# A pooled-attention kernel on one core: which half of k and q comes over which DMA queue in batch 0

## The chip, the core and the metric

The kernel runs on one core of a Trainium2 chip. The core has TensorE (PE in the profile; its weight loads are listed as PEld), VectorE (DVE), ScalarE (ACT), GpSimd (POOL) and SyncE (SP). PE multiplies matrices and writes to PSUM, DVE and ACT copy, cast and compute elementwise, POOL computes and issues DMAs, SP here only issues DMAs. The metric is the time of one execution on the device in microseconds; a lower time is better. The number given for a kernel is the median over its runs.

## What is computed

The inputs are q, k and v of 8 batches, 8 heads, 576 tokens and 64 values per head, all fp32, and two weights. First comes an attention in which k and v are averaged over groups of 8 tokens, so each head has 72 keys; then a feed-forward layer whose activation is h times cos(h). Cut to what matters:

```python
k_p = k.reshape(B, H, Sp, pool, D).mean(axis=3)          # 576 tokens -> 72
v_p = v.reshape(B, H, Sp, pool, D).mean(axis=3)
scores = scale * np.matmul(q, k_p.transpose(0, 1, 3, 2))
attn = np.exp(scores - np.max(scores, axis=-1, keepdims=True))
attn = attn / (np.sum(attn, axis=-1, keepdims=True) + 1e-09)
x = np.matmul(attn, v_p)                                 # -> (4608 tokens, 512)
h = x @ w_in                                             # 512 -> 2048
out = (h * np.cos(h)) @ w_out                            # 2048 -> 512
```

## The kernel before

The feed-forward layer is worked off in nine chunks of 512 tokens. Eight of them are the first 512 tokens (in an order of their own) of the eight batches, the ninth collects the 64 tokens left over from each batch. For each chunk PE computes h in PSUM (`up_mm`, line 348), ACT takes the cosine (line 355), DVE multiplies (line 358), and PE multiplies with w_out (line 361). The attention of the next batch is worked in between these products, and the loads, the pooling and the transposes of later batches run on POOL and SP meanwhile. Batch 0 has nothing to hide behind: its attention is the beginning of the kernel, and the first `up_mm` waits for it.

The instructions stand on each engine in the order in which the program text names them. No planner moves them; semaphores are set where one engine uses what another wrote. So a waiting instruction holds up everything that the text puts behind it on that engine.

What happens at the beginning, engine by engine, with lines of the profile:

- q, k and v of batch 0 are read so that a partition holds nine consecutive tokens of one head (`even_view`, line 85). 128 partitions hold two heads, and the four pairs of heads are the index j. "First half" means j = 0 and 1, "second half" j = 2 and 3. `load_even` (line 88) loads over POOL's queue and casts from fp32 to bf16 in the DMA. What comes over SP's queue is kept in fp32 and lands in a part of `g_sb`, the buffer of the activations, that nothing else uses yet.
- SP issues k's first half and k's second half (line 405), both fp32. ACT casts pair 0, DVE pairs 1, 2 and 3 (line 407) into the tile `kv_st`.
- POOL makes two small index tables (lines 413 and 416), then issues q's first half, q's second half, v's first half and v's second half (lines 418 to 421), then makes the identity matrix, then goes on with the eight loads of w_in (line 130) and with batch 1. From the ninth of its transfers on, each issue waits until the eighth before it has landed.
- DVE fills the tile of ones for the warm-up products (line 397), builds `groups`, a matrix of zeros and ones that says which token belongs to which group of eight (lines 427 to 431), and clears some tiles (lines 434 to 441).
- PE runs ten warm-up products of 512 columns whose result nobody uses (`warm_up`, line 472). Then `pool_k_mm` pools k's first half by multiplying with `groups` (line 180, 36 products), and DVE and ACT copy the result to `kk` (line 186). After three more warm-ups `q_transpose_mm` (line 231) transposes nine blocks of 128 columns of q's first half. The copies of these to `qT` go to ACT for four blocks and to DVE for five (line 232). After two more warm-ups come the scores of units 0 and 1 (`scores`, line 251): heads 0 to 3, tokens 0 to 255 and 256 to 511. ACT takes their exponentials (line 261).
- Then the same for the second halves: `pool_k_mm` of pairs 2 and 3, the transposes of blocks 9 to 17, the sums of the exponentials (line 280), the pooling of v (`pool_v_mm`, line 195, copied to `vz` in line 197), the scores of units 2 and 3, the products with v (line 289), the normalisation (lines 295, 296 and 303), and the first `up_mm`.

PSUM is used as three pairs of banks, `banks[0]` to `banks[2]`, and two single ones, `obanks[0]` and `obanks[1]`. Before, the pooled k of the first half lies in the two single ones, and the transposes of blocks 5 to 8 go to `obanks[0]` as well, those of 0 to 4 to a half of `banks[2]`.

Of the kernel before, what the change touches and what calls it, by code (L numbers as in the profile page):

```python
# [9 lines left out]
FP32 = mybir.dt.float32  # L10
# [9 lines left out]
def kernel(  # L20
# [9 lines left out]
    nc = tc.nc  # L30
    B, H, S, D = q.shape
# [5 lines left out]
    KCH = d_model // 128  # L37
    FFCH = d_ff // 128
    NT = n_tokens // TILE
    ROW = S // 64  # L40
# [24 lines left out]
    g_sb = wpool.tile([128, FFCH, TILE], BF16, name="g_sb")  # L65
# [11 lines left out]
    banks = [psum.tile([128, 2, 512], FP32, name=f"bank{i}") for i in range(3)]  # L77
    obanks = [psum.tile([128, 512], FP32, name=f"obank{i}") for i in range(2)]
# [4 lines left out]
    staged = {}  # L83

    def even_view(src, b, j0=0, j1=KCH):
        return src[b, 2 * j0:2 * j1].rearrange("(j a) (p t) d -> (a p) j (t d)", a=2, t=ROW)

    def load_even(dst, b, src, j0=0, j1=KCH):
        nc.gpsimd.dma_start(out=dst[:, j0:j1].rearrange("p j t d -> p j (t d)"), in_=even_view(src, b, j0, j1))
# [12 lines left out]
    def q_tile(b):  # L102
        staged["q", b] = qst.tile([128, KCH, ROW, D], BF16, name="q_b", tag="q_b")
# [69 lines left out]
    def pool_k_mm(b, pair, pj0, pj1):  # L173

        kb = staged["k", b]
        ps = [bank[:, 0:(pj1 - pj0) * Sp].rearrange("p (j n) -> p j n", n=Sp) for bank in pair]
        for pj in range(pj0, pj1):
            for t in range(ROW):
                for a, rows in enumerate(half):
                    nc.tensor.matmul(ps[a][rows, pj - pj0, :], lhsT=kb[rows, pj, t, :], rhs=groups[rows, t, :],  # L180
                                     start=(t == 0), stop=(t == ROW - 1))
        dst = kk[b % 2].rearrange("p (j a) n -> p j a n", a=2)

        def put(copy, a):
            for rows in half:
                copy(out=dst[rows, pj0:pj1, a, 0:Sp], in_=ps[a][half[a]])

        return [lambda copy, a=a: put(copy, a) for a in range(2)]
# [26 lines left out]
    def qT_tile(b):  # L215
        att["qT", b] = asb.tile([128, QB, 128], BF16, name="qT", tag="qT")

    def q_flat(b):
        return staged["q", b].rearrange("p j t d -> p (j t d)")
# [5 lines left out]
    def q_transpose_mm(b, bank, g0, g1):  # L225

        if ("qT", b) not in att:
            qT_tile(b)
        ps = bank.bitcast(BF16)[:, 0:(g1 - g0) * 128].rearrange("p (g n) -> p g n", n=128)
        for g in range(g0, g1):  # L230
            nc.tensor.matmul(ps[:, g - g0, :], q_flat(b)[:, g * 128:(g + 1) * 128], identity, is_transpose=True)  # L231
        return lambda copy: copy(out=att["qT", b][:, g0:g1, :], in_=ps)  # L232
# [166 lines left out]

    kv_even_tiles(0)  # L400
    q_tile(0)
    first_k = []
    k_first = g_sb.rearrange("p f n -> p (f n)").bitcast(FP32)[:, 0:KCH * ROW * D]
    for j in (0, 2):
        nc.sync.dma_start(out=k_first.rearrange("p (j n) -> p j n", j=KCH)[:, j:j + 2], in_=even_view(k, 0, j, j + 2))
    for j, copy in enumerate((nc.scalar.copy,) + (nc.vector.tensor_copy,) * 3):
        first_k.append(lambda j=j, copy=copy: copy(out=staged["k", 0][:, j].rearrange("p t d -> p (t d)"),  # L407
                                                   in_=k_first[:, j * ROW * D:(j + 1) * ROW * D]))
    first_k[0]()

    row_of = consts.tile([128, ROW], FP32, name="row_of")
    for rows in half:
# [2 lines left out]
    first_of = consts.tile([128, Sp], FP32, name="first_of")  # L415
    nc.gpsimd.iota(first_of, pattern=[[POOL, Sp]], base=0, channel_multiplier=0,
                   allow_small_or_imprecise_dtypes=True)
    load_even(staged["q", 0], 0, q, 0, 2)
    load_even(staged["q", 0], 0, q, 2, 4)
    load_even(staged["v", 0], 0, v, 0, 2)  # L420
    load_even(staged["v", 0], 0, v, 2, 4)
# [7 lines left out]
    nc.vector.scalar_tensor_tensor(out=sign, in0=dist, scalar=1.0 - POOL, in1=dist, op0=ADD,  # L429
                                   op1=mybir.AluOpType.mult)  # L430
    nc.vector.tensor_scalar(out=groups, in0=sign, scalar1=0.0, scalar2=None, op0=mybir.AluOpType.is_le)
    first_k[1]()
    ones = consts.tile([128, 32], BF16, name="ones")
    nc.vector.memset(ones, float(POOL))
    gate = consts.tile([1, 1], BF16, name="gate")
# [33 lines left out]
    def warm_up(n, bank):  # L469

        for i in range(n):
            nc.tensor.matmul(bank, lhsT=warm[:, 0:128], rhs=warm)  # L472

    vec, act = nc.vector.tensor_copy, nc.scalar.copy
    us = BY_HEADS

    def unit(bank):
        return bank.rearrange("p (q e n) -> p q e n", q=1, e=2)

    warm_up(10, banks[1][:, 0, :])  # L480
    puts = pool_k_mm(0, obanks, 0, 2)
    puts[0](vec)
    puts[1](act)
    first_k[2]()
    first_k[3]()
    warm_up(3, banks[1][:, 0, :])
    q_transpose_mm(0, obanks[0], 5, 9)(act)
    q_transpose_mm(0, banks[2][:, 0, :], 0, 5)(vec)
    warm_up(2, banks[1][:, 0, :])
    scores(0, us[0], banks[0])  # L490
    scores(0, us[1], banks[1])
# [41 lines left out]
    for t in range(NT):  # L533
# [76 lines left out]
        elif b < B:  # L610
# [5 lines left out]
            d = 2 if t == 1 else 0  # L616
# [84 lines left out]
```

## Time and profile before

The three runs took 292.49, 292.79 and 292.93 us, median 292.79. One execution was taken with the profiler; what follows is from it.

| | |
|---|---|
| the profiled execution's own time | 292.54 us |
| its span (first to last instruction) | 290.5 us |
| PE busy | 282.9 us, 97% of the span |
| DVE busy | 170.6 us, 59% |
| POOL busy | 145.5 us, 50% |
| ACT busy | 142.0 us, 49% |
| mean DMA rate | 127 GB/s |
| the first `up_mm` (line 348) starts at | 16.90 us |

Times inside the profile are counted from the start of the span. In the timeline a line has the start, the busy time, the engine, the source line, the operation, the tile written and the tiles read, the count, and in brackets the idle time of the engine before and what ended it. Landings of DMAs are listed separately, as the time from issue to landing. The busy time of pipelined products overlaps: 56 products of line 348 take 12.31 us together, though one lasts 0.379.

### The profile page before, as it was taken

Reading aid. Unit: us, or ns where it says so; the run is one execution under the profiler, and the core shown is the slowest. Engines: PE = TensorE matmul, PEld = TensorE weight load, DVE = VectorE, ACT = ScalarE, POOL = GpSimd, SP = SyncE. Lnnn points to the kernel's source line nnn. Section 1 sums busy time; section 2 is a strip of 40 time slices with the busy share of each in tenths; the row PEclk is TensorE's granted clock in tenths of the full one; section 3 lists DMA queues with packets and bytes.
Section 4 is the critical chain, followed back from the end, with each engine's and each line's share of the span. In section 5 each row is a group of like instructions: output and inputs, shape, how many; then the busy total and the mean of one; then the engine's idle time right before and its main releaser. Section 6 shows DMA issues by size and latency. Waiting matters only on the chain.

```text
span 290.5 us, 4941 instructions
## 1 busy us (share of the span) xinstructions
PE 282.9 (97%) x1991; PEld 147.1 (51%) x1991; DVE 170.6 (59%) x231; ACT 142.0 (49%) x142; POOL 145.5 (50%) x121
## 2 busy tenths in 40 slices
PE   7799999999999999999999999999999999999994
PEld 3555544555555555555555545554555455445443
DVE  5557885774747574658275737573666557217621
ACT  3686644679046903692368316850676066016400
POOL 8546928989964696479535982599000000000000
PEclk9999999999999999999999999999999999999999
DMA  7999999989677978695769866965703510230033
GB/s 203 197 202 210 206 203 193 166 148 212 120 147 106 190 111 174 101 176 109 158 78 198 126 138 118 185 128 105 144 1 73 119 38 0 53 82 11 0 72 73
DMA packets 57158, 36.89 MB, mean 127 GB/s; under 512 B 36400, under 2 KB 50928, under 8 KB 57136
## 3 DMA queue, kind: packets, MB, share of 16 engines
q0 software_dynamic: 17104, 17.77, 37.8%
q1 hardware_dynamic: 39792, 18.69, 33.2%
q8 instruction: 15, 0.25, 0.3%
q10 hardware_dynamic: 240, 0.13, 0.2%
q14 instruction: 7, 0.06, 0.1%
HBM read 36.70 MB, written 9.44 MB: 159 GB/s over the span
## 4 chain that ended last, share of the span: by engine, by line
PE 95%; DVE 2%; ACT 1%; issue 0%; DVEq 0%
PE bank L348 43%; PE obank L361 27%; PE bank L361 8%; PE obank L367 5%; PE bank L251 3%; PE bank L320 3%; PE bank L367 2%; PE bank L472 2%; PE bank L389 1%; PE bank L289 1%; ACT ex L261 1%; DVE qT L232 0%; DVE xT L303 0%; PE obank L180 0%; DVE kv_st L407 0%; PE obank L231 0%
## 5 line engine op out<-in xcount | busy, mean ns | idle before, releaser
L355 ACT ACTIVATE cos<-bank,half_pi 128x1024 f32<-128x1024 f32 x72 | 80.3, 1117 | 116.2 <-PE bank L348 116.2
L348 PE MATMUL bank<-xT,w_in_sb 128*128 128x512 bf16 x576 | 126.0, 379 | 0.0
L358 DVE TENSOR_TENSOR g_sb<-bank,cos 128x1024 bf16<-128x1024 f32 x72 | 88.1, 1224 | 49.1 <-ACT cos L355 49.0
L348 PEld LDWEIGHTS <-w_in_sb 128*128 128x128 bf16 x576 | 65.1, 113 | 59.1 <-issue 0.2
L361 PE MATMUL obank<-w_out_sb,g_sb 128*128 128x512 bf16 x360 | 83.9, 379 | 0.0
L361 PEld LDWEIGHTS <-g_sb 128*128 128x128 bf16 x462 | 41.9, 97 | 45.9 <-issue 2.0
L161 POOL TENSOR_TENSOR kv_st<-kv_st 72x2048 f32<-72x2048 bf16 (+1 forms) x13 | 50.4, 3877 | 14.0 <-DMA kv_st<-in_k_dram 13.9
L374 DVE COPY o_sb<-obank 128x512 f32<-128x512 f32 x21 | 14.4, 690 | 31.5 <-PE obank L361 25.9
L261 ACT ACTIVATE ex<-bank 72x1024 bf16<-72x1024 f32 x32 | 30.3, 1018 | 4.9 <-PE bank L251 4.9
L164 POOL TENSOR_TENSOR kv_st<-kv_st 72x1024 f32<-72x1024 f32 (+1 forms) x13 | 29.2, 2249 | 0.9
L361 PE MATMUL bank<-w_out_sb,g_sb 128*128 128x512 bf16 x102 | 27.6, 380 | 0.0
L324 DVE TENSOR_TENSOR x_r<-bank,inv_r 128x512 bf16<-128x512 f32 (+1 forms) x32 | 22.1, 689 | 1.3 <-DVE inv_r L321 0.3
L367 PE MATMUL obank<-w_out_sb,g_sb 64*128 64x512 bf16 x144 | 18.3, 376 | 0.0
L168 POOL TENSOR_TENSOR kp<-kv_st 72x512 bf16<-72x512 f32 (+1 forms) x14 | 16.1, 1169 | 0.5
L367 PEld LDWEIGHTS <-g_sb 64*128 64x128 bf16 x196 | 9.8, 94 | 7.3
L251 PE MATMUL bank<-qT,kk 64*72 64x256 bf16 (+1 forms) x184 | 13.0, 250 | 0.6 <-DVE qT L232 0.3
L251 PEld LDWEIGHTS <-kk 64*72 64x72 bf16 x192 | 8.4, 111 | 8.5 <-issue 3.8
L529 POOL COPY gate<-kk 1x1 bf16<-1x1 bf16 x5 | 0.9, 177 | 23.0 <-DMA kk<-kp 23.0
L119 POOL DMA_DIRECT2D kv_st<-in_v_dram x15 | 9.7, 661 | 4.8 <-DVE vz L171 4.5
L320 PEld LDWEIGHTS <-ex 72*128 72x128 bf16 x192 | 8.7, 97 | 6.2 <-ACT ex L261 1.7
L321 DVE RECIPROCAL inv_r<-bank 128x8 f32<-128x8 f32 (+1 forms) x32 | 6.5, 203 | 8.0 <-PE bank L320 7.5
L376 DVE COPY o_sb<-obank 128x512 f32<-128x512 f32 x6 | 4.1, 691 | 11.9 <-PE obank L367 11.9
(79 smaller groups left out, 167.0 us busy)
## 6 DMA issues: line engine op xcount, KB each, us to landing
out_dram<-o_sb SPq DMA_DIRECT2D x70, 128.0 KB, 2.4
q_b<-in_q_dram POOLq DMA_DIRECT2D x6, 576.0 KB, 8.2
kv_st<-in_k_dram POOLq DMA_DIRECT2D x6, 512.0 KB, 5.9
kv_st<-in_v_dram POOLq DMA_DIRECT2D x6, 512.0 KB, 10.0
w_in_sb<-in_moe_w_in_dram POOLq DMA_DIRECT2D x8, 256.0 KB, 10.7
w_out_sb<-in_moe_w_out_dram POOLq DMA_DIRECT2D x8, 256.0 KB, 10.1
g_sb<-in_k_dram SPq DMA_DIRECT2D x2, 576.0 KB, 4.0
q_b<-in_q_dram POOLq DMA_DIRECT2D x4, 288.0 KB, 8.8
```

What stands on the lines that cost most here:

```text
L161: add(out=s, in0=x[:, :, 0:4, :], in1=x[:, :, 4:8, :], op=ADD)
L164: add(out=s[:, :, 0:2, :], in0=s[:, :, 0:2, :], in1=s[:, :, 2:4, :], op=ADD)
L168: add(out=kp[:, h0:h1, slot, :], in0=s[:, :, 0, :], in1=s[:, :, 1, :], op=ADD)
L251: nc.tensor.matmul(ps.rearrange("p (g n) -> p g n", n=64), lhsT=kk[b % 2][half[r], h0 + i, 0:Sp], rhs=att["qT", b][half[r], g:g + n // 64, ...
L261: nc.scalar.activation(out=ex[:, c:c + m * w].rearrange("p (a n) -> p a n", a=m), in_=src, func=ACTF.Exp, scale=scale / POOL)
L320: nc.tensor.matmul(out[:, o0:o0 + D + 1], lhsT=ex[:, c:c + 128], rhs=v1)
L324: nc.vector.tensor_mul(out=x[:m].rearrange("p e h d -> p h e d"), in0=vals, in1=scale_of)
L348: nc.tensor.matmul(h[:, j, :], lhsT=w_in_cols(ki, fc), rhs=xT[:, ki % 2, ki // 2, t * TILE:(t + 1) * TILE], start=(ki == 0), stop=(ki == K ...
L355: nc.scalar.activation(out=cos, in_=h, func=ACTF.Sin, bias=half_pi[:, :1])
L358: nc.vector.tensor_mul(out=g_sb[:, 2 * fp:2 * fp + 2, :], in0=h, in1=cos)
L361: nc.tensor.matmul(o, lhsT=g_sb[:, fc, ms * 128:(ms + 1) * 128], rhs=w_out_sb[fc // 4][:, fc % 4, :], start=(fc == 0), stop=(fc == FFCH - 1))
L367: nc.tensor.matmul(ps, lhsT=g_sb[rows, fc, ms * 128:(ms + 1) * 128], rhs=w_out_sb[fc // 4][rows, fc % 4, :], start=start, stop=stop)
```

## The change

SP's two transfers are now the first half of k and the first half of q, both fp32, side by side in the same part of `g_sb`. POOL's first two transfers are the second half of k and the second half of q, cast in the DMA; v follows as before. k's pairs 0 and 1 are cast by ACT and DVE as before; the casts of pairs 2 and 3 on DVE are gone. q's first half, 1152 columns, is cast by two engines: ACT takes the first 448 columns and DVE the other 704. Both casts stand in the text ahead of the copies of the pooled k on these engines. One of the three warm-ups behind the pooling of k is left out. The transposes of blocks 5 to 8 go to `banks[2]`, those of 0 to 4 to `banks[0]`, so `obanks[0]` is no longer used for them, and on PE blocks 5 to 8 still come first.

```diff
-    first_k = []
-    k_first = g_sb.rearrange("p f n -> p (f n)").bitcast(FP32)[:, 0:KCH * ROW * D]
-    for j in (0, 2):
-        nc.sync.dma_start(out=k_first.rearrange("p (j n) -> p j n", j=KCH)[:, j:j + 2], in_=even_view(k, 0, j, j + 2))
-    for j, copy in enumerate((nc.scalar.copy,) + (nc.vector.tensor_copy,) * 3):
-        first_k.append(lambda j=j, copy=copy: copy(out=staged["k", 0][:, j].rearrange("p t d -> p (t d)"),
-                                                   in_=k_first[:, j * ROW * D:(j + 1) * ROW * D]))
-    first_k[0]()
+    first = g_sb.rearrange("p f n -> p (f n)").bitcast(FP32)[:, 0:KCH * ROW * D].rearrange("p (i n) -> p i n", i=2)
+    for i, src in enumerate((k, q)):
+        nc.sync.dma_start(out=first[:, i].rearrange("p (j n) -> p j n", j=2), in_=even_view(src, 0, 0, 2))
+
+    q01 = staged["q", 0][:, 0:2].rearrange("p j t d -> p (j t d)")
+
+    def first_k(copy, j):
+        n = ROW * D
+        copy(out=staged["k", 0][:, j].rearrange("p t d -> p (t d)"), in_=first[:, 0, j * n:j * n + n])
+
+    def first_q(copy, t0, t1):
+        copy(out=q01[:, t0 * D:t1 * D], in_=first[:, 1, t0 * D:t1 * D])
+
+    first_k(nc.scalar.copy, 0)
...
-    load_even(staged["q", 0], 0, q, 0, 2)
+    load_even(staged["k", 0], 0, k, 2, 4)
     load_even(staged["q", 0], 0, q, 2, 4)
...
-    first_k[1]()
+    first_k(nc.vector.tensor_copy, 1)
...
+    first_q(act, 0, 7)
+    first_q(vec, 7, 18)
     warm_up(10, banks[1][:, 0, :])
     puts = pool_k_mm(0, obanks, 0, 2)
     puts[0](vec)
     puts[1](act)
-    first_k[2]()
-    first_k[3]()
-    warm_up(3, banks[1][:, 0, :])
-    q_transpose_mm(0, obanks[0], 5, 9)(act)
-    q_transpose_mm(0, banks[2][:, 0, :], 0, 5)(vec)
+    warm_up(2, banks[1][:, 0, :])
+    q_transpose_mm(0, banks[2][:, 0, :], 5, 9)(act)
+    q_transpose_mm(0, banks[0][:, 0, :], 0, 5)(vec)
     warm_up(2, banks[1][:, 0, :])
```

## The prediction

> **What bounds the kernel now.** I read the share of busy time first: TensorE (PE) works 282.9 of 290.5 us, so there are only 7.6 us to win, and a gap on PE counts if all that follows moves with it. I then read the chain that ended last, restricted to the first 30 us, because the whole change lies there:
>
> ```profile
> 5.92 0.96 PE obank L180 x36
> 6.88 0.29 DVE kk L186
> ...
> 7.52 0.89 DVE kv_st L407 x2
> 8.41 0.38 PE obank L231 x4
> 8.79 0.29 PE bank L231 x5
> 9.11 0.50 DVE qT L232
> 9.65 0.42 PE bank L251 x4
> ```
>
> The columns are start, duration and what ran. The chain goes from the pooling of k (L180) through VectorE (DVE) to the transposes of q (L231), the copy of their result (L232) and the first scores (L251). It names the two casts of k on DVE, but they are not the only thing that ends at 8.4. The timeline of the same stretch shows the other one in brackets (idle time before, and what ended it):
>
> ```profile
> 6.77 0.82 PE L472 MATMUL bank<-warm 128*128 128x512 bf16 x3
> 7.52 0.88 DVE L407 CAST kv_st<-g_sb 128x576 bf16<-128x576 f32 x2
> 8.39 0.51 PEld L231 LDWEIGHTS <-q_b 128*128 128x128 bf16 x9 [1.29 <-DMA q_b<-in_q_dram]
> 8.91 0.59 PE L472 MATMUL bank<-warm 128*128 128x512 bf16 x2
> 9.11 0.49 DVE L232 COPY qT<-bank 128x640 bf16<-128x640 bf16 x1 [0.71 <-PE bank L231]
> 12.30 0.69 PE L195 MATMUL bank<-kv_st,groups 64*72 64x128 bf16 x18
> 13.13 0.41 DVE L197 CAST vz<-bank 72x256 bf16<-72x256 f32 x1
> 16.90 12.31 PE L348 MATMUL bank<-xT,w_in_sb 128*128 128x512 bf16 x56
> ```
>
> The weight load of the transposes waits for the DMA of q. The issue table, taken over narrow stretches so that each row is one transfer, gives the time from issue to landing in its last column:
>
> ```profile
> g_sb<-in_k_dram SPq DMA_DIRECT2D x1, 576.0 KB, 3.5
> ...
> g_sb<-in_k_dram SPq DMA_DIRECT2D x1, 576.0 KB, 4.5
> q_b<-in_q_dram POOLq DMA_DIRECT2D x1, 288.0 KB, 6.9
> ...
> q_b<-in_q_dram POOLq DMA_DIRECT2D x1, 288.0 KB, 7.5
> kv_st<-in_v_dram POOLq DMA_DIRECT2D x1, 288.0 KB, 8.2
> ```
>
> With the issue times of the timeline (SP at 0.75 and 1.27, POOL at 1.41, 2.29, 3.02 and 3.84) the landings are: SP's first 4.25, SP's second 5.77; POOL's first 8.31, second 9.8, first of v 11.2, second of v about 12.6. The first q half lands at 8.31, PE starts its weights at 8.39. That the casts of k end at 8.40 is a coincidence: the first transposes need obanks[0], which DVE had read by 7.49. So PE stands from 7.59 to 8.39 for the transfer.
>
> **The change part by part.**
>
> **Transfers.** SP still issues two transfers of the same shape (0.97 us for both), POOL still four, in the same places of its queue; nothing is inserted ahead of the loads of w_in. So I carry each landing over by its place: k's first half 4.25, q's first half 5.77 (was 8.31), k's second half 8.31 (was 5.77), q's second half 9.8, v 11.2 and 12.6, all as before. Nothing waits on SP behind these two issues until a transpose at 48.29.
>
> **Casts.** Removed: two casts of k on DVE, 0.88 us from 7.52, behind the first kk copies. They delay nothing on PE, so I count nothing for them. Added: q's first 448 columns on ScalarE (ACT) and the other 704 on DVE. By width, from 672 ns for 576 columns on ACT, 448 cost 0.52 us; from 505 ns for 576 on DVE, 704 cost 0.62 us. The bounds are 460 and 672 ns, the quickest and slowest of these casts, scaled to 704 columns: 0.56 to 0.82 us. Both engines are free by 5.5 (DVE's last memset at 5.02 takes 0.48), so both wait for 5.77 and end by 6.4 to 6.65. Behind them stand the copies of kk (L186), which wait for PE's 6.88 anyway. Cover: 0.23 us or more; if it is gone, kk and the first scores slip by the excess.
>
> **PE's start of the transposes.** Three warm-ups become two. They begin at 6.77 and follow each other at 0.216 us (0.59 for two less 0.38 for one), so the transposes can begin at 6.77 + 2 x 0.216 = 7.20, when the q casts are 0.5 us or more old. Before it was 8.39, so the start moves by 1.19 us. The same nine transposes take 0.68 (8.39 to 9.07). Now the four for ACT come first; ACT is done with its kk copies at 7.47 and copies them from 7.64 to 8.22. DVE copies the five from 7.92 to 8.41, the first scores start at 8.45 instead of 9.65. This step is worth **1.20 us**. More is not to be had, because PE is then busy without a gap.
>
> **What is late next.** Every PE step that follows is asked for 1.20 us earlier; I compare with the landings. The pooling of k's second half is asked for at 10.21 - 1.20 = 9.01 and has its data at 8.31. The transposes of q's second half, asked for at 9.71, get theirs at 9.8; their copies queue on DVE behind four kk copies until 11.2, which hides the 0.1. The pooling of v's first half (L195) is asked for at 11.10, but v lands at 11.2 and is seen 0.08 later, as q was: 11.30. It takes 0.69, its copy to vz (L197) starts at 12.03 instead of 11.93, and the scores of unit 3 reuse its bank. So about **0.10 us** is given back. If the landing is 0.1 earlier the loss is nothing; if all queued POOL transfers came as late as their next place in the queue (v at 12.6, its copy at 13.41), 1.48 us would be lost, more than the gain. I take the measured places, since neither size nor order changes. Later landings have more room: v's second half 12.6 against 13.8; w_in's first 13.9 against 15.7; its fourth (7.43 + 10.8 = 18.2) against about 19.5; q of batch 1 (16.30 + 10.1 = 26.4) against 27.6. From 17 us on the waits of PE name no DMA, so I see nothing that takes the microsecond back.
>
> **Sum.** 292.54 us is the profiled execution's own time (span 290.5 and 2.0 around it), 0.25 below the median of the runs shown, 292.79. 292.54 - 1.20 + 0.10 = 291.44; from the median the same difference gives 291.69. I say **291.65 us**, 0.4% less.
>
> **A rule against it.** The table of DMA queues (packets, MB, share of the 16 engines), taken from 1.7 to 4.9 us, has one row:
>
> ```profile
> q1 hardware_dynamic: 476, 1.06, 93.3%
> ```
>
> That is SP's queue. POOL's is missing, though POOL had issued three transfers by 3.85. The Trainium skill, "DMA: Bandwidth & Descriptors", section "Queues, rings and completion order", says that each DMA engine takes turns between the queues that have work, packet by packet; its section on issuing engines adds that another issuing engine saves only issue time. By that, SP's second transfer would share the engines with POOL's first and both would land near each other, the gain shrinking to the difference in issue, by my estimate from that page 1.41 - 1.27 = 0.14 us, a time of 292.65. The trace shows another order, and I go by it.
>
> **The rivals.**
>
> *Late q, slower.* The cast of q now heads DVE's queue ahead of the kk copies, and if the first half of q lands late, kk, transposes and scores all wait. With the cast of 0.62 and two hand-overs of 0.06 the transposes start 0.74 after the landing. So a landing up to 6.46 costs nothing, at 7.65 all the gain is gone, at 8.31 (where POOL's first landed) PE starts at 9.05 and the time is 292.79 + 0.66 = 293.45. Against it: SP's second transfer landed at 5.77 although the same POOL transfers were queued beside it.
>
> *Cold clock, slower.* The granted clock reads 1.00 in every window, so the durations must tell. The first ten warm-ups run for 634 ns each and start every 0.427 us, later ones 379 ns and every 0.216. One warm-up fewer, and dense short work, could let the slow rate return; each 512-column product at the slow rate costs 0.21 us, so six undo the gain and nine make the kernel slower. Against it: PE stood idle for 0.80 us before without losing the fast rate, and now stands less. With 16 slow products: 291.65 + 3.4 = 295.0. The skill's "TensorE: Matmul & The Clock Gate", Part 4, says that transposes do not count as busy work for the clock, which would speak for this rival; the 379 ns of the two warm-ups right after nine transposes speak against it.
>
> *Absorbed, same.* The start moves but POOL's queue holds PE at v or at q's second half: with both 0.8 us later than before, 292.4.
>
> *The change hides nothing*, because the casts of k and not the DMA bound the transposes: excluded as a loss, since both leave the path together.
>
> **How the numbers follow.** Forecast (gain 0.9 to 1.3) 0.70; partly absorbed (0.2 to 0.9) 0.15; nothing won 0.05; slower by late q 0.06, by clock or unknown 0.04. About 0.2%, 0.59 us, is what a measurement of this kernel can tell. Faster takes the forecast and half of the partly absorbed: 0.77; same 0.13; slower 0.10. The forecast's own range is 291.3 to 292.0. The range for 8 in 10 adds most of the absorbed cases: 291.2 to 292.5; what lies outside is the slower cases and a rest on either side.
>
> **What would show it.** L231's first weight load at 7.2 without a wait for a DMA; first L251 at about 8.45; L195 at 11.1 to 11.3, waiting for v; first L348 at about 15.8 instead of 16.90, and the end of the span the same 1.1 earlier, at 289.4. The prediction is wrong if q's cast starts well after 5.8, if products of 512 columns after 7 us take 634 ns, or if the gap at 7.6 comes back at 11.

## The result, and the profile after

The changed kernel takes 291.46 us (median of 6 runs, 291.31 to 291.75) against 292.82 us for the kernel before (6 runs, 292.49 to 293.04) beside it. The ratio is 0.9956, with a 95% interval from 0.9943 to 0.9969. The prediction said 291.65. Run twice more among the experiments, the same pair gave 0.9957 (0.9945 to 0.9968) and 0.9969 (0.9959 to 0.9980). One of the kernels below (k's second half as a third transfer on SP) had three of its twelve executions at 296.39 to 296.83 us with a mean granted clock of 0.98, and its ratio is taken from the other nine. The profiled execution took 291.31 us, its span is 289.6.

The chain that ended last in the first part of the changed kernel (start, duration, what) no longer goes through the transposes of q:

```profile
1.43 0.87 POOL kv_st L89
2.30 0.45 POOL q_b L89
2.75 0.27 issue
3.02 8.28 DMA kv_st<-in_v_dram
11.30 0.04 issue
11.34 0.71 PE bank L195 x18
...
12.14 0.43 DVE vz L197
12.57 0.04 issue
12.62 0.41 PE bank L251 x4
13.03 0.58 PE bank L289 x16
```

It begins with POOL's issues, runs 8.28 us through the DMA of v's first half, and reaches PE only at 11.34, with the pooling of v. The wait has moved by one tensor: from q's first half to v's first half. The timeline of the changed kernel shows what PE did before that. The brackets hold the idle time before and what ended it (a selection of its lines):

```profile
5.83 0.77 PE L180 MATMUL obank<-groups,kv_st 64*64 64x72 bf16 x36
5.93 0.57 ACT L413 CAST q_b<-g_sb 128x448 bf16<-128x448 f32 x1 [0.77 <-DMA g_sb<-in_q_dram]
5.93 0.53 DVE L413 CAST q_b<-g_sb 128x704 bf16<-128x704 f32 x1 [0.17 <-DMA g_sb<-in_q_dram]
6.97 0.67 PE L231 MATMUL bank<-identity,q_b 128*128 128x128 bf16 x9
8.22 0.63 PE L251 MATMUL bank<-qT,kk 64*72 64x256 bf16 x8
9.91 0.68 PE L231 MATMUL bank<-identity,q_b 128*128 128x128 bf16 x9 [0.37 <-DMA q_b<-in_q_dram]
11.34 0.69 PE L195 MATMUL bank<-kv_st,groups 64*72 64x128 bf16 x18 [0.41 <-DMA kv_st<-in_v_dram]
12.14 0.42 DVE L197 CAST vz<-bank 72x256 bf16<-72x256 f32 x1 [0.42 <-PE bank L195]
12.62 0.41 PE L251 MATMUL bank<-qT,kk 64*72 64x256 bf16 x4 [0.36 <-DVE vz L197]
15.92 4.03 PEld L348 LDWEIGHTS <-w_in_sb 128*128 128x128 bf16 x20 [0.21 <-issue]
```

The transposes begin at 6.97 instead of 8.39 with no wait for a DMA, and the scores at 8.22 instead of 9.65: 1.43 us earlier. The pooling of v begins at 11.34 instead of 12.30, only 0.96 earlier, and the first weights of L348 at 15.92 instead of 16.90. The last stage of the kernel (line 389, the final 128 tokens) starts at 281.69 instead of 282.66: 0.97. So 1.43 was won at the scores and 0.46 given back at v; nothing else is lost on the way to the last stage. The second half of q also held PE up, for 0.37 us at 9.91, but that cost nothing: PE was ready for the pooling of v at 11.34 - 0.41 = 10.93 and v had not landed.

The issue table of the changed kernel, over narrow stretches so that each row is one transfer (last column: us from issue to landing):

```profile
g_sb<-in_k_dram SPq DMA_DIRECT2D x1, 576.0 KB, 3.7
...
g_sb<-in_q_dram SPq DMA_DIRECT2D x1, 576.0 KB, 4.6
kv_st<-in_k_dram POOLq DMA_DIRECT2D x1, 288.0 KB, 7.0
...
q_b<-in_q_dram POOLq DMA_DIRECT2D x1, 288.0 KB, 7.6
...
kv_st<-in_v_dram POOLq DMA_DIRECT2D x1, 288.0 KB, 8.3
```

With the issues at 0.75, 1.28, 1.41, 2.29 and 3.02 the halves land at 4.45, 5.88, 8.41, 9.89 and 11.32. Each place in a queue kept its landing within 0.2 us, whichever tensor it carried.

### The profile page after: what moved, and what is told of

It is laid out like the page before. It is cut to its first block, busy times and chain, and to the rows that moved or that the text cites. A ratio compares the mean times of both kernels' runs of the same rounds, so it can differ in the third digit from the quotient of the medians.

```text
span 289.6 us, 4905 instructions
## 1 busy us (share of the span) xinstructions
PE 279.0 (96%) x1956; PEld 146.8 (51%) x1990; DVE 170.5 (59%) x230; ACT 142.7 (49%) x143; POOL 145.3 (50%) x121
## 4 chain that ended last, share of the span: by engine, by line
PE 89%; DMA 3%; DVE 3%; ACT 2%; issue 1%; POOL 1%; DVEq 0%; POOLq 0%
PE bank L348 40%; PE obank L361 25%; PE bank L361 7%; PE obank L367 5%; PE bank L251 3%; DMA kv_st<-in_v_dram 3%; PE bank L320 3%; PE bank L367 2%; DVE g_sb L358 2%; ACT cos L355 2%; PE bank L389 1%; PE bank L289 1%; DVE xT L303 0%; POOL kv_st L89 0%; DVE vz L197 0%
## 5 line engine op out<-in xcount | busy, mean ns | idle before, releaser
L348 PE MATMUL bank<-xT,w_in_sb 128*128 128x512 bf16 x565 | 125.3, 379 | 0.7 <-issue 0.2
L348 PEld LDWEIGHTS <-w_in_sb 128*128 128x128 bf16 x576 | 65.1, 113 | 59.1 <-issue 0.2
L361 PE MATMUL obank<-w_out_sb,g_sb 128*128 128x512 bf16 x346 | 82.3, 379 | 0.5
L361 PE MATMUL bank<-w_out_sb,g_sb 128*128 128x512 bf16 x94 | 26.0, 379 | 1.2 <-issue 1.1
## 6 DMA issues: line engine op xcount, KB each, us to landing
w_out_sb<-in_moe_w_out_dram POOLq DMA_DIRECT2D x8, 256.0 KB, 10.1
```

What stands on the lines that cost most here:

```text
L348: nc.tensor.matmul(h[:, j, :], lhsT=w_in_cols(ki, fc), rhs=xT[:, ki % 2, ki // 2, t * TILE:(t + 1) * TILE], start=(ki == 0), stop=(ki == K ...
L361: nc.tensor.matmul(o, lhsT=g_sb[:, fc, ms * 128:(ms + 1) * 128], rhs=w_out_sb[fc // 4][:, fc % 4, :], start=(fc == 0), stop=(fc == FFCH - 1))
```

## The experiments

My theory after this comparison: the transposes of q started earlier because q's first half now comes over SP; and v's landing at about 11.3 is what PE waits for next. Rivals: one warm-up fewer or the free bank made the gain; the casts are on the path; ACT or DVE, not v, set the rest. The questions after those: could v come earlier, or matter less, and what lets SP's two transfers go ahead of POOL's?

### Transfers and casts undone, the rest of the change kept

```diff
-    warm_up(3, banks[1][:, 0, :])
-    q_transpose_mm(0, obanks[0], 5, 9)(act)
-    q_transpose_mm(0, banks[2][:, 0, :], 0, 5)(vec)
+    warm_up(2, banks[1][:, 0, :])
+    q_transpose_mm(0, banks[2][:, 0, :], 5, 9)(act)
+    q_transpose_mm(0, banks[0][:, 0, :], 0, 5)(vec)
```

(against the kernel before)

> The queues and casts are those of before (all of k's first load over SP, q over POOL, k's pairs 2 and 3 cast on DVE); the two warm-ups and the new banks of the transposes are kept. Theory (the gain comes from q's first half landing at 5.9 instead of 8.3): PE waits for q again, L231 starts at about 8.4, and the time is that of before, 292.8 +- 0.2. Rival (one warm-up fewer or the free obanks[0] made the gain): L231 starts before 7.8 and the time stays below 292.2.

Measured: 292.47 against 292.52 us, ratio 0.9999 (0.9990 to 1.0007). The chain of this kernel shows the old wait:

```profile
1.42 6.80 DMA q_b<-in_q_dram
8.21 0.04 issue
8.26 0.69 PE bank L231 x9
8.95 0.02 issue
8.97 0.50 DVE qT L232
9.48 0.04 issue
9.52 0.63 PE bank L251 x8
```

PE stands until q lands. The warm-up and the banks are worth nothing by themselves; the gain comes from the queues, with the casts that belong to them. The run also settles a doubt of the prediction: here the chain names the DMA, no longer the casts of k on DVE that happened to end at the same moment before. In this execution they end at 7.86 (0.86 us from 7.00), and PE still waits until 8.26.

### Three warm-ups again in the changed kernel

```diff
-    warm_up(2, banks[1][:, 0, :])
+    warm_up(3, banks[1][:, 0, :])
```

> The changed kernel with three warm-ups behind the pooling of k instead of two. Theory (v's first half, landing at 11.3, is now what PE waits for, and about 0.2 to 0.4 us of the earlier start is idle): the transposes start 0.22 later but L195 still starts at 11.3 and the time is that of the changed kernel within 0.1 us, 291.5. Rival (the start of the transposes still sets the end): 0.22 us slower, 291.7.

> The changed kernel with three warm-ups again, beside the changed kernel itself on one chip. If v's landing alone sets the end: no difference within 0.1 us. If the fast clock of the products comes late in some executions, so that the start of the transposes sets the end there: a mean loss between 0 and 0.22 us, about 0.1.

Measured: 291.68 us, 0.9970 (0.9959 to 0.9981) in the first set, which had no run of the changed kernel in it; and 291.26 in the last set, where the changed kernel took 291.52, ratios to before 0.9962 (0.9950 to 0.9974) and 0.9969. The third warm-up costs PE 0.22 us and the median nothing that can be measured. Lines from the timeline of the first of these kernels show how little room is left:

```profile
5.85 0.95 PE L180 MATMUL obank<-groups,kv_st 64*64 64x72 bf16 x36
7.39 0.67 PE L231 MATMUL bank<-identity,q_b 128*128 128x128 bf16 x9
11.28 0.69 PE L195 MATMUL bank<-kv_st,groups 64*72 64x128 bf16 x18
```

Here PE reaches the pooling of v at 11.28 and need not wait, since v came early in this execution, at 3.03 + 7.8 = 10.8. So in this one the start of the transposes set the rest, and the third warm-up counted. In the second run it did not: PE came to v earlier and waited for it, until 11.02.

### q's first half cast by one engine

```diff
-    first_q(act, 0, 7)
-    first_q(vec, 7, 18)
+    first_q(vec, 0, 18)
```

> The changed kernel with q's first half cast by DVE alone, 1152 columns. By the measured 0.53 us for 704 columns this takes 0.87, from 5.93 to 6.80. Theory (the cast has cover, and 0.2 to 0.4 us behind it are idle for v): the copies of kk on DVE move by 0.2, the transposes by at most 0.1, and the time is that of the changed kernel within 0.1 us, 291.5. Rival (the casts are on the path, and two engines are needed): 0.2 to 0.4 us slower, 291.7 to 291.9.

> q's first half cast by DVE alone, again beside the changed kernel on one chip. Theory (the cast has cover, v's landing sets the end): within 0.1 us of the changed kernel. Rival (two engines are needed): 0.2 to 0.4 us slower.

Measured: 291.58 us, 0.9966 (0.9955 to 0.9977), and in the last set 291.40 beside 291.52 of the changed kernel. In the first of them PE does wait for the cast, and for v all the same (lines from its timeline):

```profile
6.82 0.68 PE L231 MATMUL bank<-identity,q_b 128*128 128x128 bf16 x9 [0.24 <-DVE q_b L413]
9.82 0.68 PE L231 MATMUL bank<-identity,q_b 128*128 128x128 bf16 x9 [0.41 <-DMA q_b<-in_q_dram]
11.30 0.69 PE L195 MATMUL bank<-kv_st,groups 64*72 64x128 bf16 x18 [0.46 <-DMA kv_st<-in_v_dram]
```

The 0.24 us of waiting at the transposes cost nothing, because PE then waits another 0.46 for v. In the second run the cast ends at 6.93 (0.76 us from 6.17) and the transposes start at 7.51, behind the warm-ups. Two engines for the cast are not needed here.

### v's first half not loaded

```diff
-    load_even(staged["v", 0], 0, v, 0, 2)
...
     q_transpose_mm(0, banks[0][:, 0, :], 0, 5)(vec)
+    vec(out=staged["v", 0][:, 0:2].rearrange("p j t d -> p (j t d)"), in_=first[:, 1])
```

> The changed kernel without the load of v's first half in batch 0. In its place DVE casts the fp32 copy of q's first half into the same tile at about 8.2 us, in time for PE, so heads 0 to 3 of batch 0 use wrong values of v; all work on the engines stays, plus one cast of 0.9 us. Theory (v's landing took the rest of the gain): L195 starts when it is asked for, at about 10.9, without a wait, the first L348 about 0.4 earlier than in the changed kernel (about 15.5 instead of 15.9), time 291.1. Rival (ACT's exponentials or DVE's copies of qT set the rest of the chain): no change, 291.5.

Measured: 291.09 us, 0.9954 (0.9940 to 0.9968). The other two kernels of this set that kept the changed queues had 0.9970 and 0.9966, so it is 0.5 to 0.6 us below them, with intervals that overlap. The traces are clearer:

```profile
9.46 0.68 PE L231 MATMUL bank<-identity,q_b 128*128 128x128 bf16 x9 [0.24 <-DMA q_b<-in_q_dram]
10.07 0.54 PE L280 MATMUL bank<-ex,ones 72*32 72x256 bf16 x8
10.54 0.69 PE L195 MATMUL bank<-kv_st,groups 64*72 64x128 bf16 x18
...
280.89 3.70 PE L389 MATMUL bank<-w_out_sb,g_sb 128*128 128x256 bf16 x48
```

Without the load, the pooling of v starts at 10.54 with no wait, and the last stage starts 0.80 before that of the changed kernel. Of that, 0.34 is an earlier start of this execution (its transposes began at 6.63 instead of 6.97); the other 0.46 is v. PE still waited 0.24 for q's second half here, and the pooling of v began no later for it.

### The changed kernel again

> The changed kernel itself, beside the others of this set on one chip, so that they can be compared with it. 1.1 to 1.4 us less than before.

> The changed kernel itself on the chip of this set, for comparison: 1.2 to 1.4 us less than before.

Measured: 291.31 us, 0.9957, and 291.52 us, 0.9969. That is 1.36 and 0.99 us less than before; the second is below what I expected.

These traces together give the main reading of the study. Each row is one profiled execution, times in us: the start of the first transposes (L231), the same plus 3.90, the landing of v's first half by the issue table (issue plus time to landing, to 0.1 us), the start of the pooling of v's first half (L195; bold where the brackets show PE waiting for its DMA), the start of the last stage, and the difference of the last two.

| kernel | L231 | L231 + 3.90 | v landed | L195 | last stage | difference |
|---|---|---|---|---|---|---|
| before | 8.39 | 12.29 | 11.2 | 12.30 | 282.66 | 270.36 |
| transfers undone | 8.26 | 12.16 | 11.1 | 12.17 | 282.54 | 270.37 |
| changed | 6.97 | 10.87 | 11.3 | **11.34** | 281.69 | 270.35 |
| changed, second | 7.06 | 10.96 | 11.0 | 11.05 | 281.39 | 270.34 |
| changed, third | 7.17 | 11.07 | 11.3 | **11.31** | 281.66 | 270.35 |
| three warm-ups | 7.39 | 11.29 | 10.8 | 11.28 | 281.67 | 270.39 |
| three warm-ups, second | 6.81 | 10.71 | 10.9 | **11.02** | 281.36 | 270.34 |
| one engine | 6.82 | 10.72 | 11.2 | **11.30** | 281.63 | 270.33 |
| one engine, second | 7.51 | 11.41 | 10.9 | 11.41 | 281.76 | 270.35 |
| v not loaded | 6.63 | 10.53 | not loaded | 10.54 | 280.89 | 270.35 |

From the pooling of v on, everything takes the same time, 270.33 to 270.39 us. Where L231 + 3.90 comes after v, L195 starts within 0.01 of it (before, transfers undone, three warm-ups, one engine's second, and the kernel without the load); where v lands later, L195 starts within about 0.1 of the landing. In the trace of before these 3.90 us run through the first scores (9.65), ACT's exponentials (10.10 to 12.03) and their sums (12.08). So the time is set by the later of two things: the start of the transposes plus 3.9, and the landing of v, which scatters from 10.8 to 11.3 between executions with the same queues. Before, it was the first; after, mostly the second.

### Unit 3 in the single banks

```diff
-    scores(0, us[3], banks[1])
+    scores(0, us[3], tuple(obanks))
...
-    scores_mm(0, REST, tuple(obanks))
-    s23 = [ob[:, 256:512] for ob in obanks]
+    rest0 = banks[1][:, :, 0:256]
+    scores_mm(0, REST, rest0)
+    s23 = [banks[1][:, i, 256:512] for i in range(2)]
...
-    scores_exp(0, REST, tuple(obanks))
+    scores_exp(0, REST, rest0)
```

> The changed kernel with the scores of unit 3 in the two single banks, which are free by then, and the scores of the 64 rest tokens and two sums in banks[1] instead; so unit 3 no longer waits until the pooled v has been copied out of banks[1]. Theory (v's landing costs its time through that bank): scores of unit 3 follow those of unit 2 at once, at about 12.2 instead of 12.6; the products with v (L289) start when vz is copied, about 0.3 earlier, and the time is 0.2 to 0.4 us below the changed kernel's. Rival (ACT, whose exponentials of unit 3 become two instructions and 0.2 us longer, sets the end): no gain or 0.2 us slower.

Measured: 291.16 us, 0.9956 (0.9944 to 0.9968), beside 291.31 and 0.9957 of the changed kernel: the same. The local step came as foreseen. Unit 3 followed unit 2 at 11.82, and L348 began at 15.34 instead of 15.63. But 39 products of L348 then took 8.90 us instead of 8.64, and the last stage began at 281.37 instead of 281.39. The timeline shows ACT reading banks[1] until 16.45, where the second pair of up products wants to write:

```profile
15.87 0.58 ACT L261 ACTIVATE ex_rest<-bank 72x512 bf16<-72x512 f32 x1
...
16.50 1.41 PEld L348 LDWEIGHTS <-w_in_sb 128*128 128x128 bf16 x7 [0.36 <-issue]
```

I read this as the gain becoming a new wait on the same bank. It is not shown: the profile puts that wait of the weight loads down to issue and not to ACT, and the next experiment, which was to test it, ran into another wait.

### The rest tokens' exponential moved ahead

```diff
     s23 = [banks[1][:, i, 256:512] for i in range(2)]
+    scores_exp(0, REST, rest0)
...
-    scores_exp(0, REST, rest0)
```

(against the kernel with unit 3 in the single banks)

> The kernel with unit 3 in the single banks, with the exponential of the rest tokens moved on ACT to directly behind those of unit 3, ahead of the inverses; so banks[1] comes free at about 15.75 instead of 16.45 us. Theory (the 0.3 us that unit 3 in the single banks won at L289 were lost again because the second pair of up products waited for banks[1]): 39 products of L348 take 8.64 again instead of 8.90, and the time is 0.2 to 0.35 us below the changed kernel's of this set. Rival (the gain at L289 is lost elsewhere, by ACT's longer chain to the second half of xT): no gain over the changed kernel.

Measured: 295.18 us, 1.0089 (1.0077 to 1.0101) of before: 3.7 us slower than the changed kernel of this set, a clear miss. All five executions took 294.25 us or more. First a wait on PE (us in all, times, longest):

```profile
PE bank L280 <- ACT ex_rest L261: 1.3, 1, 1.3
```

In the text the exponential now stands ahead of the sums of units 2 and 3. These write other columns of the same banks[1], and PE waits until ACT has read it. ACT gets to that read only behind three other exponentials, at 14.08. That accounts for 1.32 us, and so the theory could not be tested. The rest goes with the clock. The table by windows (us; PE, PEld, DVE, ACT and POOL busy with counts; granted PE clock; DMA share; GB/s) has it:

```profile
13.40:14.70 1.30, 0.01 (x2) 0.03 (x1) 1.17 (x2) 1.28 (x3) 0.17 (x1) 0.98 1.24 202
14.70:17.80 3.10, 2.82 (x42) 1.62 (x41) 0.42 (x1) 1.12 (x4) 1.84 (x3) 0.50 1.24 205
17.80:21.50 3.70, 3.70 (x13) 1.32 (x10) 1.29 (x2) 1.66 (x2) 1.53 (x3) 0.50 1.24 206
21.50:30.00 8.50, 8.50 (x40) 4.42 (x39) 5.18 (x5) 5.47 (x5) 5.95 (x9) 1.00 1.14 210
```

At the end of the stall the granted clock falls to 0.50 and stays there until 21.5. In that time a product of 512 columns takes 631 ns instead of 379, and one starts every 0.427 us instead of every 0.216. By these rows: 1.32 for the stall, 0.48 and 0.43 for L195 (1.17 instead of 0.69) and L289 (1.05 instead of 0.62), and 3.7 / 0.427 = 8.7 slow products at 0.21 each, 1.8: together 4.0, as an estimate. The distance from L195 to the last stage was 270.27 in the kernel with unit 3 in the single banks and is 274.09 here, 3.8 more.

### k's second half as a third transfer on SP

```diff
-    first = g_sb.rearrange("p f n -> p (f n)").bitcast(FP32)[:, 0:KCH * ROW * D].rearrange("p (i n) -> p i n", i=2)
-    for i, src in enumerate((k, q)):
-        nc.sync.dma_start(out=first[:, i].rearrange("p (j n) -> p j n", j=2), in_=even_view(src, 0, 0, 2))
+    first = g_sb.rearrange("p f n -> p (f n)").bitcast(FP32)[:, 0:6 * ROW * D].rearrange("p (i n) -> p i n", i=3)
+    for i, (src, j) in enumerate(((k, 0), (q, 0), (k, 2))):
+        nc.sync.dma_start(out=first[:, i].rearrange("p (j n) -> p j n", j=2), in_=even_view(src, 0, j, j + 2))
...
-        copy(out=staged["k", 0][:, j].rearrange("p t d -> p (t d)"), in_=first[:, 0, j * n:j * n + n])
+        copy(out=staged["k", 0][:, j].rearrange("p t d -> p (t d)"), in_=first[:, j // 2 * 2, j % 2 * n:j % 2 * n + n])
...
-    load_even(staged["k", 0], 0, k, 2, 4)
...
     q_transpose_mm(0, banks[0][:, 0, :], 0, 5)(vec)
+    first_k(vec, 2)
+    first_k(act, 3)
```

> The changed kernel with k's second half as a third fp32 transfer on SP, cast by DVE (pair 2) and ACT (pair 3) behind their copies to qT; POOL's first transfers are then q's second half and v. Theory A (POOL's packets start only when SP's stream is through, so the order of the halves and the bytes ahead of v stay as they are): k's second half lands at about 7.3, q's second half at 9.9, v at 11.3, and the time is the changed kernel's within 0.2 us. Theory B (POOL's first transfer has a lag of its own of about 1 us, which would now lie beside SP's third): v at about 10.5 and 0.3 to 0.4 us less.

Measured: ratio 0.9991 (0.9982 to 1.0000), so nearly all of the gain is gone, and neither theory had the landings right. In this kernel SP's third transfer was issued at 1.76:

```profile
g_sb<-in_q_dram SPq DMA_DIRECT2D x1, 576.0 KB, 4.7
g_sb<-in_k_dram SPq DMA_DIRECT2D x1, 576.0 KB, 8.2
q_b<-in_q_dram POOLq DMA_DIRECT2D x1, 288.0 KB, 8.7
```

It landed at 9.96, not at 7.3, and POOL's first at 10.1. PE waited for the cast of k:

```profile
10.50 0.77 PE L180 MATMUL obank<-groups,kv_st 64*64 64x72 bf16 x36 [1.17 <-DVE kv_st L410]
```

The table of queues of this kernel from 1.7 to 5.4 has SP's row alone; from 6 to 8 it has both:

```profile
q0 software_dynamic: 178, 0.21, 59.5%
q1 hardware_dynamic: 158, 0.35, 52.1%
```

q0 is POOL's queue, q1 SP's. The MB are as written, so POOL's 0.21 MB of bf16 are 0.42 MB read. Two transfers, one from each queue, share the engines about evenly, and both come late. The pooling of v began at 12.76, and 270.36 later the last stage.

### q's first half over POOL, k alone on SP

```diff
-    for i, src in enumerate((k, q)):
+    for i, src in enumerate((k,)):
...
+    load_even(staged["q", 0], 0, q, 0, 2)
     load_even(staged["k", 0], 0, k, 2, 4)
...
-    first_q(act, 0, 7)
-    first_q(vec, 7, 18)
```

> The changed kernel with only k's first half on SP and q's first half as POOL's first transfer, cast in the DMA; k's second half, q's second half and v follow on POOL. Nothing is left out. Theory A (the halves come in the order in which they are issued, whatever the queue, and only SP's bytes hold POOL's back): q's first half lands at about 6.9, L231 starts at about 7.0 to 7.2 and the time is the changed kernel's within 0.2 us. Theory B (POOL's first transfer has a lag of its own): q lands at about 8.3 as in the kernel before and the time is 0.8 to 1.2 us above the changed kernel's. If the two queues took turns packet by packet, k's first half would land later than 4.5 in the kernels with two transfers on SP than here.

Measured: 291.85 us, 0.9968 (0.9956 to 0.9980), beside 291.31 of the changed kernel. That is 0.54 more, between the two theories. POOL's first transfer was issued at 1.42 and landed after 6.3 us, at 7.7: 0.6 earlier than behind two transfers of SP, not 1.4. Over 3.6 to 4.8 us, when SP's one transfer ends, POOL's packets have set in, but move little:

```profile
q0 software_dynamic: 71, 0.08, 89.4%
q1 hardware_dynamic: 42, 0.06, 13.3%
```

These 71 packets took 89% of the engines' time for 0.08 MB. The first of them ran between 3.6 and 3.8; in the changed kernel, with two transfers on SP and POOL's first issued at 1.41, the first ran between 5.0 and 5.2. So both theories hold in part: POOL's packets do wait for SP's stream, and its first transfer is slow by itself. v, now fourth in POOL's queue, landed at 3.74 + 8.3 = 12.04 and the pooling of v began at 12.08, 1.03 later than in the changed kernel of this set. By the sum of the table q would have allowed 7.76 + 3.90 = 11.66; v came later and set the rest:

```profile
7.76 0.68 PE L231 MATMUL bank<-identity,q_b 128*128 128x128 bf16 x9 [0.24 <-DMA q_b<-in_q_dram]
...
12.08 0.69 PE L195 MATMUL bank<-kv_st,groups 64*72 64x128 bf16 x18 [0.35 <-DMA kv_st<-in_v_dram]
```

The distance to the last stage was 270.35 again. The time of the profiled execution shows less of the 1.03, 291.87 against 291.24; part of the rest lies behind the start of the last stage, 7.6 us to the end of the span here and 7.8 there, and no trace says why. The third comparison of the expectation decides nothing: k's first half landed at 0.75 + 3.5 = 4.25 here, and at 4.25, 4.45 and 4.55 in three traces with two transfers on SP (before, changed, changed again).

## Why the prediction was right

- **What bounds the kernel.** Right. PE's stand from 7.59 to 8.39 was the DMA of q; with the queues put back it returns.
- **Landings carried over by place.** Right: 4.45, 5.88, 8.41, 9.89 and 11.32 against 4.25, 5.77, 8.31, 9.8 and 11.2.
- **Casts.** 0.57 and 0.53 us against 0.52 and 0.62, both done by 6.5. The cover was smaller than I said, 0.17 us in place of 0.23 or more (the copies of kk follow at 6.63 and 6.67), because the pooling of k ended earlier. Even so 1152 columns on one engine cost nothing at the end, because v hides it.
- **Start of the transposes.** Predicted 7.20 and worth 1.20 us; measured 6.97, 7.06 and 7.17 in three executions. The scatter comes from the pooling of k ahead of it, which takes 0.77 us in some executions and up to 1.29 in others, as PE's products go from 634 to 379 ns earlier or later. The prediction carried over the 0.99 of one execution. It makes little difference where v lands later.
- **What is late next.** The right transfer, mis-sized. The term "about 0.10 us is given back" was 0.46 in the profiled execution, 0.36 more: about 0.23 because PE came earlier, 0.04 because the pooling of v began at 11.34 and not 11.30, and 0.10 because I put the copy to vz 0.73 us behind the start of that pooling, where the trace before has 0.83 (12.30 to 13.13) and the one after 0.80. The constant 270.35 shows that nothing on the way hides v's delay. Rightly worked, the step would have given 12.30 - 11.30 = 1.00 instead of 1.10. The profiled pair shows 0.97. In the other two traces of the changed kernel, beside the same trace of before, 0.06 and 0.22 were given back.
- **The sum.** 291.65 against 291.46, inside the stated range and the forecast's own. Three sets gave differences of 1.36, 1.36 and 0.99 us; the predicted 1.14 lies among them. That it is so near is in part luck: the two errors above, 0.23 more won and 0.36 more given back, nearly cancel. And of the 1.23 us between the two profiled executions 0.3 lies outside the span (292.54 - 290.5 = 2.0 before, 291.31 - 289.6 = 1.7 after), where no trace shows anything.
- **The rule against it.** The landing order of the prediction held: in the changed kernel, too, only SP's packets ran from 1.7 to 4.9 us (470 of them). The Trainium skill's "DMA: Bandwidth & Descriptors", section "Queues, rings and completion order", has the engines take turns between the queues that have work. In this stretch the traces do not agree with that: the POOL transfer issued at 1.42 had packets from 3.6 to 3.8 on where SP had one transfer, and one issued at 1.41 only from 5.0 to 5.2 on where SP had two. Why is not shown. With a third transfer on SP the two queues did share, from 5.4 us on. Had the first two been shared in that way, the gain would have been small, as the prediction priced it.
- **Rivals.** The late q did not occur. Of the absorbed case a part did: 0.46 us of the 1.43, at v, where it was placed. The cold clock did not occur in the changed kernel, but it is real: in one experiment it followed on a stall of 1.32 us, at 0.21 us per product as priced.

## What to carry to other kernels

When a wait goes, look for the next landing in the same queue and put it on the same clock: PE's start plus the fixed work, or the landing, whichever is later. The gain ends at that crossing, here after 1 us of 1.43 in the profiled execution, and work that shortens only the other side (a second engine for a cast, one warm-up fewer) buys nothing beyond it. Putting one more transfer on the quick queue is not the same step again: the third shared the engines with the other queue and came 2.7 us later than the pace of the first two promised (9.96 instead of 7.3).

## What the runs showed that I had not expected

The distance from the pooling of v to the last stage is 270.33 to 270.39 us in the ten traces of the table, and 270.35 and 270.36 in the two kernels with other queues. Only the two kernels with unit 3 in the single banks differ. In a kernel so tightly ordered, the start of one early stage measures a change to what stands ahead of it better than the total time, which scatters by 0.5 us and more.

An idle time of PE of 1.32 us, between stretches of short products, was followed by a granted clock of 0.50 for 6.8 us. In the kernel with the transfers undone, an idle time of 1.40 us (6.86 to 8.26) was not: the products behind it ran at 0.379 us. Nor was one of 1.17 us in the profiled execution of the kernel with a third transfer on SP (9.33 to 10.50), where the pooling behind it takes 0.77. What decides between these stays open. The granted clock reads 1.00 in the first 5.4 us of the run, though the warm-up products there take 634 ns, so there only the durations tell.

Why SP's first two transfers ran ahead of POOL's first, while the third did not, was not settled. POOL's first was issued at 1.41 or 1.42, between SP's second (1.28) and third (1.76), so an order of issue would fit, and so do POOL's first packets, which came when SP's transfers issued ahead of them were nearly through; no run put a POOL transfer ahead of all of SP's.
